# Fused two-stage attention and MLP on one core: a planner with other costs, joined filler matmuls, the last batch in token order, the last output tile in three pieces of columns

## The chip, the cores and the metric

The kernel runs on one core of one Trainium2 chip. The core has a matrix engine (TensorE, "PE" in the profile; its weight loads are "PEld"), a vector engine (DVE), an activation engine (ACT), GpSimd (POOL), SyncE (SP) and 16 DMA engines. The metric is device time in microseconds (us) of one execution, from one launch; lower is better. The time given for a kernel is the median of its runs.

## The reference

Eight batches, eight heads, 576 tokens of 64 numbers per head, and 32 "packed" queries `p` per head. The packed queries attend to the keys and values, then the queries attend to the packed result; the heads are put side by side to 512 columns, and an MLP with 2048 hidden columns (d_ff) follows:

```python
p_packed = sm_attn(p, k, v)            # softmax(p k^T / 8) v : 32 x 64 per head
out = sm_attn(q, p_packed, p_packed)   # softmax(q p_packed^T / 8) p_packed
x = out.transpose(0, 2, 1, 3).reshape(B * S, H * D)       # 4608 x 512
h = x @ w_in                                               # 4608 x 2048
g = where(h >= 1, h, where(h <= -1, 0, (h + 1)**2 / 4))
y = g @ w_out                                              # 4608 x 512, f32
```

## The kernel before

**Algebra.** The second attention and the first matmul of the MLP are merged: with A the normalised weights of the second softmax (transposed; 256 rows of head and packed query, in two groups g of 128) and M = p_packed w_in (256 x 2048), the hidden activations of a batch are M^T A. So per batch the kernel makes M and A, then 16 *hidden tiles* (`hidden_tile`, L541): tile `fi` is 128 columns of d_ff by the 576 tokens of the batch, four matmuls of 128x288 into PSUM (L548), `first` on ACT (L553, Prelu, PSUM to the f32 buffer `x`), `second` on DVE or ACT (L558 or L560), `third` on DVE (L563), which writes bf16 into `hT`. An *output tile* (`out_tile`, L584) is 128 tokens by 512 columns: 16 *steps*, one for each `fi`, each a 128x512 matmul that adds to one PSUM bank `o` (L598); then a copy to SBUF by ACT or DVE (`ob`, L319) and two DMAs on SP's queue (L604). Two batches share nine output tiles, so there are 36 of them and 576 steps.

**Attention of a batch** (`attention`, L357): `trans` (L376) turns k and q with matmuls on PE, twelve 96-wide ones for each half of the heads, for batches 0 to 2; from batch 3 on a transposing DMA on SP's queue does it (`turned`, L512). `scores` (L397, `sp`) and an exp on ACT (L400, `ex`); `packed` (L417 and L423, `pk`), a copy `p1`, an add and a copy that make `ppT` (L433, L435) and a reciprocal `rs` (L436); `weights` (L451, `s2`), exp on ACT (L456, `eT`), the sums (L461, `sm`), their reciprocal on ACT as ln and exp (L465, L469, `rc`) and `norm` on DVE (L472, `A`); `mk` (L493, `mp`) with a copy by ACT or DVE, which makes a quarter of M (M0 to M3, 512 columns of d_ff each). A hidden tile needs both groups of A and its quarter of M.

**Buffers.** `psW` has 3 PSUM buffers of two banks, which every product except `o` takes; `psO` has 2 banks for `o`. The `x` buffers are 5, the `ob` buffers 6. With two `o` banks, at most two output tiles are under way.

**Order.** All of the work is handed as tasks to a planner (`Plan`, L33), which is run when the program is built. It keeps a clock for each engine, takes the cost of each task and the delays between engines from the table `C` (L12), and picks the next task by start time and key; the order in which it picks is the order in which the instructions are emitted, and each engine works through its own in that order. So a change of a number in `C` can change the order of every engine's queue, but no instruction's duration on the chip. Loads go through POOL's queue in a fixed order: k, v and q of batch 0 in halves, w_in and w_out in quarters, k, v and q of batch 1, the last quarter of w_out, p, and then the later batches. While fewer than three `o` tiles have been begun and PE has nothing to do by the planner's clock, `run` (L131 to L139) emits *fillers*, 128x256 matmuls on zeros (L661), one for each 107 ns of planned idle time.

**Rows of the output.** A load puts six neighbouring tokens of a head into one partition, so the kernel's token order is not the output's: token 6t + 2e + x of a batch stands at x * 288 + e * 96 + t. `out_rows` (L573) cuts a tile into pieces in which t runs on, up to 96 rows, each of which is one DMA with every sixth row of the output as its target.

**The last output tile** (`end`, L588) has two accumulators of 256 columns, one in the bank of `o` and one in a `psW` buffer (`o2`), and each step is two 128x256 matmuls. `done_last` (L606) copies one half on ACT and one on DVE, and each of the two engines' queues (ACT's and SP's) sends two DMAs, of 96 and 32 rows.

## Time and profile before

| | |
|---|---|
| runs shown | 252.23 us median of three (251.41, 252.23, 252.58) |
| the profiled execution | 250.97 us, of which the span from the first to the last instruction is 249.2 us |
| PE, ACT, DVE busy | 94%, 73%, 73% of the span |
| granted clock of TensorE | 1.00 throughout |
| output DMAs | 72 issues on SP's queue and 2 on ACT's |

The profile is one execution. A row of a timeline or of the chain of waits gives the start in us from the span's start, the duration in us, the engine, the line of the kernel, the instruction and its tiles, and how many instructions are merged; in square brackets stands the engine's idle time before it and what ended it. A matmul's duration holds its way through the array, so the distance between two starts, and not the duration, is what a matmul costs in a stream of them.

### The profile page before, as it was taken

The numbers are of one execution on the slowest core, as the hardware profiler recorded it, in microseconds if no ns is written. First come the engines' busy times: TensorE is split into PE (matmuls) and PEld (weight loads), VectorE is DVE, ScalarE is ACT, GpSimd is POOL, SyncE is SP. The second block draws the span as 40 slices with busy tenths as digits, with TensorE's granted clock in tenths as the row PEclk, the third lists the DMA queues.
The fourth block names the chain that finished last, engine by engine and source line by source line (L and its number), as shares of the span: only waits on it lengthen the run. The fifth ranks groups of instructions, "written<-read, shape, count | busy, mean of one in ns | idle before, by whom it ended". The sixth has DMA issues, their size and how long they took to land.

```text
span 249.2 us, 5464 instructions
## 1 busy us (share of the span) xinstructions
PE 234.8 (94%) x2187; PEld 140.9 (57%) x2220; DVE 181.7 (73%) x308; ACT 182.5 (73%) x294; POOL 29.7 (12%) x44
## 2 busy tenths in 40 slices
PE   7887887999999999999999999999999999999993
PEld 5655465467546666556565656656556465544452
DVE  5456979788999899698979985998569878930000
ACT  3368888899888899798798984997859796841110
POOL 8632433012001301111101000000000000000000
PEclk9999999999999999999999999999999999999999
DMA  6999999999999999999999932312112112133223
GB/s 99 196 207 207 206 203 195 204 240 204 193 182 217 165 190 193 208 183 188 223 191 223 218 76 53 79 42 49 42 42 45 43 42 45 42 84 86 54 74 84
DMA packets 54825, 34.37 MB, mean 138 GB/s; under 512 B 27536, under 2 KB 50320, under 8 KB 54800
## 3 DMA queue, kind: packets, MB, share of 16 engines
q0 software_dynamic: 24672, 18.55, 49.9%
q1 hardware_dynamic: 29968, 15.34, 31.7%
q8 instruction: 17, 0.28, 0.4%
q10 hardware_dynamic: 160, 0.13, 0.2%
q14 instruction: 8, 0.07, 0.1%
HBM read 37.22 MB, written 9.44 MB: 187 GB/s over the span
## 4 chain that ended last, share of the span: by engine, by line
PE 76%; DMA 13%; ACT 3%; POOL 3%; issue 2%; DVE 2%; DVEq 0%; ACTq 0%; POOLq 0%
PE o L598 44%; PE h L548 22%; DMA w_in_sb<-in_moe_w_in_dram 7%; DMA q<-in_q_dram 6%; PE mp L493 3%; PE sp L397 2%; PE pk L417 1%; PE sm L461 1%; PE s L451 1%; PE tp L376 1%; DVE pT L319 1%; POOL w_in_sb L285 1%; ACT eT L456 1%; POOL k L259 1%; PE pk L423 1%
## 5 line engine op out<-in xcount | busy, mean ns | idle before, releaser
L598 PE MATMUL o<-w_out_sb,hT 128*128 128x512 bf16 (+1 forms) x559 | 135.6, 373 | 2.1 <-issue 1.1
L563 DVE SCALAR_TENSOR_TENSOR hT<-x 128x576 bf16<-128x576 f32 x128 | 93.2, 754 | 8.3 <-PE o L598 3.5
L598 PEld LDWEIGHTS <-hT 128*128 128x128 bf16 x592 | 56.1, 98 | 53.7 <-issue 4.8
L553 ACT ACTIVATE x<-h 128x576 f32<-128x576 f32 x128 | 77.2, 653 | 12.1 <-PE h L548 8.3
L548 PE MATMUL h<-A,M 128*128 128x288 bf16 x512 | 76.0, 286 | 1.4 <-ACT M L319 0.5
L548 PEld LDWEIGHTS <-M 128*128 128x128 bf16 x512 | 49.3, 98 | 24.1 <-ACT M L319 1.0
L558 DVE TENSOR_SCALAR x<-x 128x576 f32<-128x576 f32 x84 | 38.5, 459 | 11.8 <-ACT x L553 10.9
L319 ACT COPY ob<-o 128x512 f32<-128x512 f32 (+1 forms) x23 | 13.2, 576 | 32.1 <-PE o L598 32.1
L560 ACT ACTIVATE x<-x 128x576 f32<-128x576 f32 x44 | 29.4, 683 | 0.5
L319 DVE COPY ob<-o 128x512 f32<-128x512 f32 (+1 forms) x14 | 9.4, 669 | 25.8 <-PE o L598 25.7
L319 DVE CAST M<-mp 128x1024 bf16<-128x1024 f32 x16 | 19.4, 1218 | 2.8 <-PE mp L493 2.8
L319 ACT CAST M<-mp 128x1024 bf16<-128x1024 f32 x16 | 15.8, 1012 | 1.2 <-PE mp L493 1.2
L400 ACT ACTIVATE ex<-sp 96x768 bf16<-96x768 f32 x16 | 12.9, 806 | 3.2 <-PE sp L397 3.1
L472 DVE SCALAR_TENSOR_TENSOR A<-eT,rs,rc 128x576 bf16<-128x576 bf16 x16 | 13.0, 812 | 2.1 <-ACT rc L469 2.1
L259 POOL DMA_DIRECT2D k<-in_k_dram x10 | 7.5, 746 | 56.5 <-DMA kT<-k 40.0
L456 ACT ACTIVATE eT<-s,rs 128x576 bf16<-128x576 f32 x16 | 11.2, 736 | 2.8 <-PE s L451 2.6
L493 PE MATMUL mp<-w_in_sb,ppT 64*32 64x512 bf16 x256 | 10.7, 381 | 2.6 <-DMA w_in_sb<-in_moe_w_in_dram 2.2
L465 ACT ACTIVATE ln<-sm 128x576 f32<-128x576 f32 x16 | 10.4, 648 | 2.2 <-PE sm L461 2.1
L661 PE MATMUL o<-zeros 128*128 128x256 bf16 x68 | 10.6, 301 | 1.2 <-DVE zeros L247 1.2
L469 ACT ACTIVATE rc<-ln 128x576 f32<-128x576 f32 x16 | 10.9, 683 | 0.5
L259 POOL DMA_DIRECT2D q<-in_q_dram x10 | 7.6, 759 | 26.2 <-DMA qT<-q 12.7
L397 PEld LDWEIGHTS <-kT 128*128 128x128 bf16 x192 | 7.4, 98 | 2.6 <-DVE kT L319 0.6
(47 smaller groups left out, 114.4 us busy)
## 6 DMA issues: line engine op xcount, KB each, us to landing
out_dram<-ob SPq DMA_DIRECT2D x23, 192.0 KB, 2.5
v<-in_v_dram POOLq DMA_DIRECT2D x7, 576.0 KB, 18.4
k<-in_k_dram POOLq DMA_DIRECT2D x6, 576.0 KB, 12.4
q<-in_q_dram POOLq DMA_DIRECT2D x6, 576.0 KB, 14.0
out_dram<-ob SPq DMA_DIRECT2D x24, 128.0 KB, 2.8
w_in_sb<-in_moe_w_in_dram POOLq DMA_DIRECT2D x4, 512.0 KB, 14.7
w_out_sb<-in_moe_w_out_dram POOLq DMA_DIRECT2D x4, 512.0 KB, 16.8
out_dram<-ob SPq DMA_DIRECT2D x23, 64.0 KB, 2.0
```

Source lines behind the costliest of these rows:

```text
L259: nc.gpsimd.dma_start(tok[nm, b][:, hs].rearrange("p h c d -> p h (c d)"), SRC[nm][b, hs].rearrange("h (p c) d -> p h (c d)", c=NC))
L319: return lambda eng: nc.vector.tensor_copy(out_, in_) if eng == DVE else nc.scalar.copy(out_, in_)
L400: nc.scalar.activation(ex()[:, :, i].rearrange("p e x a n -> p e (x a n)"), box["sp"], AF.Exp, scale=scale)
L456: nc.scalar.activation(box["eT"], box["s2"][:, :, :HALF], AF.Exp, scale=rs()[:, g, 1:])
L472: nc.vector.scalar_tensor_tensor(A()[:, g], box["eT"], rs()[:, g, :1], box["rc"], ALU.mult, ALU.mult)
L493: nc.tensor.matmul(mp[a * NP:(a + 1) * NP, g], pp_of(y, h), w_in_sb[y * D:(y + 1) * D, h // 2, f * FW:(f + 1) * FW], start=True, stop=True)
L548: nc.tensor.matmul(h[:, hf, :HALF], T[b, "M"][:, g, fi * P:(fi + 1) * P], T[b, "A"][:, g, hf], start=(g == 0), stop=(g == G - 1))
L553: nc.scalar.activation(box["x"], box["h"][:, :, :HALF], AF.Prelu, bias=-1.0, alpha=0.5)
L558: nc.vector.tensor_scalar(x, x, 1.0, 0.0, ALU.add, ALU.max)
L560: nc.scalar.activation(x, x, AF.Relu, bias=1.0)
L563: nc.vector.scalar_tensor_tensor(hT[:, fi, col:col + S].rearrange("p (a t) -> p a t", a=2), box["x"], 1.0, box["x"], ALU.min, ALU.mult)
L598: nc.tensor.matmul(o, hT[:, fi, i * P:(i + 1) * P], w_out_sb[:, fi, cs], start=(fi == 0), stop=(fi == KF - 1))
```

## The change

1. **The planner's table.** `C` gets other numbers. Among them: `load` 2.95 to 3.5666, `land` 1.75 to 2.0125, `xt` 5 to 6.5, `M` 0.345 to 0.2415, `s2` 0.25 to 0.2862, `pk` 1.05 to 0.9765, `td` 0.457 to 0.489, `obd` 0.69 to 0.6276, `slack` 0.6 to 0.51, `margin` 0.15 to 0.1717, `feed` 0.1 to 0.085, `join` 0.15 to 0.1604. All of the other entries but `tell` (0.04 to 0.034) stay.
2. **Fillers.** Planned idle time is counted up and emitted ahead of PE's next task as matmuls of up to 512 columns.
3. **Last batch.** `norm` of batch 7 is two DVE instructions (one for each x) that write A in the order t, e, so that its columns are in the order of the tokens; `out_rows` then cuts at 288 rather than 96, and a DMA writes every second row of the output.
4. **Last tile.** The left 256 columns are summed first, in 16 steps, copied and sent; then the right 256 in 16 steps of two 128-column matmuls each, into two banks of one `psW` buffer, and two copies of 128 columns with one DMA each.
5. A list `cuts` is made for the first four output tiles. No other line reads it.

```diff
-C = dict(load=2.95, half=1.46, w_in=2.57, w_out=2.57, rest=1.25, out=9.0, p=4.05, land=1.75, xt=5.0, xland=11.0,
...
+C = dict(load=3.5666, half=1.46, w_in=2.57, w_out=2.57, rest=1.25, out=9, p=4.05, land=2.0125, xt=6.5, xland=11, tpp=0.06, tp=0.042, sc=0.034, pk=0.9765, s2=0.2862, sm=0.245, M=0.2415, h=0.49, o=0.217, switch=0.05, join=0.1604, pTc=0.1, Tca=1.12, Tcd=0.76, ex=0.82, ppT=0.42, ppo=0.41, ppa=0.4, ppd=0.2, rs=0.18, eT=0.74, ln=0.65, rc=0.68, A=0.82, Mca=1, Mcd=1.22, x=0.65, ta=0.683, td=0.489, hT=0.758, oba=0.585, obd=0.6276, array=0.2, wake=1.2, warm=4.2, early=0.3, tell=0.034, feed=0.085, slack=0.51, margin=0.1717, wait=0.5)
-DW = 256
+DW, FILL = 256, 512
...
-                    idle()
+                    fill += DW
                     self.now["PE"] += step
                     continue
...
+            while e == "PE" and fill:
+                w = min(fill, FILL)
+                idle(w)
+                fill -= w
...
             def norm(eng):
+                if b == B - 1:
+
+                    for x in range(X):
+                        o, e, r_ = [v.rearrange(w, e=E) for v, w in ((A()[:, g, x], "p (t e) -> p t e"),
+                                    (box["eT"][:, x], "p (e t) -> p t e"), (box["rc"][:, x], "p (e t) -> p t e"))]
+                        nc.vector.scalar_tensor_tensor(o, e, rs()[:, g, :1], r_, ALU.mult, ALU.mult)
+                    return
                 nc.vector.scalar_tensor_tensor(A()[:, g], box["eT"], rs()[:, g, :1], box["rc"], ALU.mult, ALU.mult)
...
+            if b == B - 1:
+                r = t % HALF
+                n = min(HALF - r, (i + 1) * P - t)
+                res.append((t - i * P, n, out[b * S:(b + 1) * S].rearrange("(r x) d -> x r d", x=X)[x, r:r + n]))
+                t += n
+                continue
...
-        w = d_model // 2
+
+        cuts = [12, KF] if pr == 0 and i < 4 else [KF]
+
+        w, sub = (d_model // 2, d_model // 4) if end else (d_model, d_model)
...
-            box["o2"] = wide([P, w], f32, "o2")
+            box["o2"] = wide([P, 2, FW], f32, "o2")
...
+            pieces = [(box["o2"][:, y, :sub], slice(w + y * sub, w + (y + 1) * sub)) for y in range(2)] if j else [(box["o"][:, :w], slice(w))]
+            for o, cs in pieces:
                 nc.tensor.matmul(o, hT[:, fi, i * P:(i + 1) * P], w_out_sb[:, fi, cs], start=(fi == 0), stop=(fi == KF - 1))
...
+            for y, (eng, queue) in enumerate(((ACT, nc.scalar), (DVE, nc.sync))):
+                ob = ops.tile([P, sub], f32, tag="ob" + str(y), name="ob" + str(y), bufs=1)
+                copy(ob, box["o2"][:, y, :sub])(eng)
+                for a, n, dst in out_rows(pr, i):
+                    queue.dma_start(dst[:, w + y * sub:w + (y + 1) * sub], ob[a:a + n])
+        for j in range(2 if end else 1):
+            if j:
+                prev = prev + [add(PE, 0.0, 100 + pr * NT + i, prev, spare, takes="W", readers=1)]
+            for fi in range(KF):
+                t = add(PE, C["o"] * (0.5 if end else 1.0), 100 + pr * NT + i, [wrote[b, fi] for b in bs] + prev + [L["out", fi // 4]],
+                        lambda fi=fi, j=j: step(fi, j), mode=0, takes="O" if fi == 0 and j == 0 else None, readers=1, slack=C["slack"])
...
+            if j:
+                add((DVE, ACT), {ACT: C["oba"], DVE: C["obd"]}, b_key(pr, i), prev, done_last)
+            else:
+                both(done, C["oba"], C["obd"], b_key(pr, i), prev, frees=owner, takes="ob", holds=C["out"])
```

The order that the planner makes of it, as far as the prediction speaks of it (instructions of PE in the order of its queue; "steps" are those of output tiles):

| stretch | before | after |
|---|---|---|
| fillers | 68 of 256 columns | 33 of 512 and 6 of 256 |
| ahead of the first turn of k of batch 1 | 12 hidden tiles, 18 steps | 15 hidden tiles, 17 steps |
| then, up to `pk` of batch 1 | turn, 2 tiles, turn, `sp`, step, tile, `sp`, tile, 5 steps | turn, tile, 3 steps, turn, step, `sp`, 3 steps, `sp` |
| after `pk` of batch 1 | turn q, turn q, M0, s2, s2, sm, M1, sm, step, M2, 2 steps, M3 | turn q, M0, turn q, s2, M1, M2, s2, sm, M3, step, sm |
| ACT after the exps of `sp` of batch 1 | p1, q copy, eT, eT, ln, rc, ln, rc | p1, ppT copy, M0 copy, eT, M1 copy, eT, ln, rc, ln, rc |
| steps ahead of the first hidden tile of batch 1 | 40 | 36 |
| steps between the first `s2` and the first hidden tile, batches 2 to 7 | 24, 23 and 6 tiles, 25 and 7 tiles, 21 and 6 tiles, 17, 20 | 24, 22, 22, 22, 24, 23 |

More of the change, by code (lines that the diff above doesn't have):

```diff
@@ L123, in run @@
                     given[e].append(t)
-        n = len(self.tasks)
+        n, fill = len(self.tasks), 0
         while n:
@@ L478, in weights @@
             i_ = add(ACT, C["rc"], km, [l_] + p_, inv)
-            a_ = add(DVE, C["A"], km, [i_] + K.get((b - 2, "h"), []), norm)
+            a_ = add(DVE, C["A"] + (0.1 if b == B - 1 else 0.0), km, [i_] + K.get((b - 2, "h"), []), norm)
             last["ln"] = [i_]
@@ L601, in done @@
             box["ob"] = ops.tile([P, d_model], f32, tag="ob", name="ob")
-            copy(box["ob"], box["o"])(eng)
+            copy(box["ob"][:, :w], box["o"][:, :w])(eng)
             for a, n, dst in out_rows(pr, i):
-                nc.sync.dma_start(dst, box["ob"][a:a + n])
+                nc.sync.dma_start(dst[:, :w], box["ob"][a:a + n, :w])
         def done_last(eng):
-            for j, (eng, queue, o) in enumerate(((ACT, nc.scalar, box["o"][:, :w]), (DVE, nc.sync, box["o2"]))):
-                ob = ops.tile([P, w], f32, tag="ob" + str(j), name="ob" + str(j), bufs=1)
-                copy(ob, o)(eng)
-                for a, n, dst in sorted(out_rows(pr, i), key=lambda x: -x[1]):
-                    queue.dma_start(dst[:, j * w:(j + 1) * w], ob[a:a + n])
@@ L613, in out_tile @@
-        if end:
-            prev = [add(PE, 0.0, 100 + pr * NT + i, [K[B - 1, "h"][-1]], spare, takes="W", readers=1)]
-        for fi in range(KF):
-            t = add(PE, C["o"], 100 + pr * NT + i, [wrote[b, fi] for b in bs] + prev + [L["out", fi // 4]],
-                    lambda fi=fi: step(fi), mode=0, takes="O" if fi == 0 else None, readers=1, slack=C["slack"])
-            step_of[pr, i, fi] = t
-            prev = [t]
-            if fi == 0:
-                owner = t
-        both(done_last if end else done, C["oba"], C["obd"], b_key(pr, i), prev, frees=owner, takes="ob", holds=C["out"])
+            for y, (eng, queue) in enumerate(((ACT, nc.scalar), (DVE, nc.sync))):
[3 more added lines that the diff above has]
+                    queue.dma_start(dst[:, w + y * sub:w + (y + 1) * sub], ob[a:a + n])
@@ L660 @@
     plan.count["O"] = 1
-    plan.run(lambda: nc.tensor.matmul(o[:, :DW], zeros[:, :P], zeros[:, :DW], start=True, stop=True))
+    plan.run(lambda w: nc.tensor.matmul(o[:, :w], zeros[:, :P], zeros[:, :w], start=True, stop=True))
 _INS = ['q', 'k', 'v', 'p', 'moe_w_in', 'moe_w_out']
```

13 lines of the change are left out of this document (6 added, 7 removed).

## The prediction

> **What bounds the kernel now.** I read the sums and groups of the page, then busy time in stretches of 10 us, then the chain of waits.
>
> ```profile
> span 249.2 us, 5464 instructions
> PE 234.8 (94%) x2187; PEld 140.9 (57%) x2220; DVE 181.7 (73%) x308; ACT 182.5 (73%) x294; POOL 29.7 (12%) x44
> ...
> 20.00:30.00 10.00, 8.38 (x65) 5.30 (x63) 8.03 (x15) 8.66 (x15) 2.56 (x5) 1.00 1.24 207
> 30.00:40.00 10.00, 9.32 (x137) 6.42 (x137) 8.39 (x14) 8.43 (x14) 4.07 (x5) 1.00 1.31 204
> 40.00:50.00 10.00, 8.30 (x107) 4.50 (x106) 8.36 (x13) 8.12 (x12) 1.53 (x2) 1.00 1.44 197
> 60.00:70.00 10.00, 9.79 (x82) 5.84 (x82) 9.27 (x18) 8.76 (x15) 0.45 (x1) 1.00 1.27 206
> 200.00:210.00 10.00, 9.95 (x76) 5.92 (x62) 7.57 (x13) 7.66 (x13) 0.00 (x0) 1.00 0.22 54
> ...
> 179.22 1.96 PE h L548 x16
> 192.00 3.45 PE o L598 x16
> 219.22 10.74 PE o L598 x49
> 240.80 4.53 PE o L598 x36
> ```
>
> The columns of the stretches are length, then busy time of PE, PEld, DVE, ACT and POOL, clock, DMA share and GB/s. From about 53 us on PE is 98 to 99% busy and the chain's rows follow one another on it; the last 26 us hold only steps. There the time is the count of matmuls by their spacing: a step 3.45 / 16 = 0.216 us, a hidden tile 1.96 / 4 = 0.49 us. The kernel computes as much as before, so these 190 us can't shrink by a new order; they can only get gaps. What can be won or lost lies in the first 53 us, where PE is idle (1.6, 0.7 and 1.7 us in three of the stretches), and behind the last matmul.
>
> **The first 53 us.** Loads set this part, and POOL's queue has the same order in both kernels, so I keep their landings. The rows of before:
>
> ```profile
> 25.07 0.41 PE L493 MATMUL mp<-w_in_sb,ppT 64*32 64x512 bf16 x8 [0.98 <-DMA w_in_sb<-in_moe_w_in_dram]
> 28.51 1.64 PE L548 MATMUL h<-A,M 128*128 128x288 bf16 x12 [0.49 <-ACT M L319]
> 33.59 0.68 PE L376 MATMUL tp<-ident,k 96*128 96x96 bf16 x12 [0.51 <-DMA k<-in_k_dram]
> 38.61 0.86 PE L417 MATMUL pk<-ex,v 96*128 96x64 bf16 x24
> 40.86 0.68 PE L376 MATMUL tp<-ident,q 96*128 96x96 bf16 x12 [0.58 <-DMA q<-in_q_dram]
> 49.05 0.65 PE L548 MATMUL h<-A,M 128*128 128x288 bf16 x4
> ...
> 51.38 0.51 PE tp L376 x12
> 55.52 0.35 PE sp L397 x12
> ...
> L560 ACT ACTIVATE x<-x 128x576 f32<-128x576 f32 x44 | 29.4, 683 | 0.5
> 37.44 0.80 ACT L400 ACTIVATE ex<-sp 96x768 bf16<-96x768 f32 x1
> 39.79 0.37 ACT L319 COPY p<-pk 64x256 f32<-64x256 f32 x1 [0.30 <-PE pk L423]
> 42.08 1.49 ACT L456 ACTIVATE eT<-s,rs 128x576 bf16<-128x576 f32 x2 [0.64 <-PE s L451]
> 48.00 1.02 ACT L319 CAST M<-mp 128x1024 bf16<-128x1024 f32 x1
> ...
> 46.25 0.82 DVE L472 SCALAR_TENSOR_TENSOR A<-eT,rs,rc 128x576 bf16<-128x576 bf16 x1 [0.25 <-ACT rc L469]
> ```
>
> *Up to 33.6 us.* In the new order the copy of M2 comes earlier in ACT's queue, the wait of 0.49 us at 28.51 goes, and 15 tiles and 17 steps instead of 12 and 18 stand ahead of the first turn of k. That turn waits for its load in both. So PE is ahead by 3 x 0.49 - 0.216 = 1.25 us of work.
>
> *Up to pk.* Before: 38.61 - 33.59 = 5.0 us of queue without a gap. After: two turns (0.51), one tile, seven steps and two `sp` (0.35) make 3.7 us, so PE stands at `pk` at about 37.3. But ACT's exps are no earlier: the first `sp` ends at about 36.5, then ACT does exp (0.80), a relu of a hidden tile (0.68) and exp, 36.5 + 2.3 less 0.1, by which a next one starts before an end, = 38.7. Half of `pk` needs the second exp. Nearly all of the 1.25 us is idle time here; `pk` ends at 39.4.
>
> *The second half of q.* It lands at about 40.8 (row 40.86). Before, its turn follows the first one. Now M0 stands ahead of it, and M0 waits for `ppT`: p1 (0.37), an add on DVE and a copy on ACT of about the same size, one behind the other from 39.5 on, with 0.1 between them 40.9. M0 takes 0.3 to the next start; the turn begins at 41.2, 0.3 later, and behind it in PE's queue everything else.
>
> *ACT's queue.* Now the copies of M0 and M1 (0.9 each to the next start, row 48.00) lie ahead of the first and the second `eT`. First `eT` 41.35 + 0.9 = 42.3 (42.08 before), second 43.9 (42.08 + 1.49 / 2 = 42.8 before), and from there ln, rc, ln, rc as before: A is complete at about 48.5 instead of 47.07. PE fills this with the 12 steps that are left, but with one gap, where the third output tile waits for an `ob` copy that stands behind two M copies on DVE. The first hidden tile of batch 1 then starts at about 48.7 with 36 steps done; before, at 49.05 with 40. Behind by 4 x 0.216 - 0.35 = 0.5 us.
>
> I take **+0.5 us**. Ends: -1.5, if the 1.25 us and one switch of tiling (about 0.28) are kept because ACT's exps do come earlier; +1.5, if A's delay of 1.4 us shows in full.
>
> **From 53 us to 219 us.** From batch 3 on each attention moves some 5 to 9 us of PE's work later, and no hidden tiles are left between `s2` and the first tile that needs A. By counts and spacings the distance is 22 steps, 4.75 us, and 1.1 us of other matmuls, 5.85 us for batches 3 to 5 (before 9 to 10). Is the chain shorter? Batch 6 of before had 17 steps and four M products:
>
> ```profile
> 167.64 0.37 PE s L451 x16
> 173.49 0.98 PE h L548 x8
> qT<-q SPq DMA_TRANSPOSE x10, 8.1
> ...
> 169.69 0.65 ACT L465 ACTIVATE ln<-sm 128x576 f32<-128x576 f32 x1 [0.36 <-PE sm L461]
> 172.49 0.82 DVE L472 SCALAR_TENSOR_TENSOR A<-eT,rs,rc 128x576 bf16<-128x576 bf16 x1 [0.58 <-ACT rc L469]
> ```
>
> From `s2` to the end of A it took 173.31 - 167.64 = 5.67 us, to the tile 5.85, without a wait of PE. The new batches have the same distance, so 0.2 us to spare: I take **+0.1** for all, 0 to +2 as ends (0.4 for each of five batches). The turning DMAs go out later on SP's queue, the second q of batch 4 behind output tile 9; that is still 20 us of PE's queue ahead of its `s2`, and a landing takes 8.
>
> **Fillers.** 72 x 256 columns instead of 68. Ahead of loads they end where the load lands; one unit more delays batch 0's A by 0.1 us, which the wait of 0.98 us at 25.07 takes up: 0. Without that wait 0.1.
>
> The rows for the two edits at the end:
>
> ```profile
> 245.25 0.37 ACT L319 COPY ob<-o 128x256 f32<-128x256 f32 x1 [2.75 <-PE o L598]
> 245.36 0.42 DVE L319 COPY ob<-o 128x256 f32<-128x256 f32 x1 [24.50 <-PE o L598]
> 245.65 0.86 ACTq L612 DMA_DIRECT2D out_dram<-ob  x2
> 245.81 0.79 SPq L612 DMA_DIRECT2D out_dram<-ob  x2
> L319 DVE COPY ob<-o 128x512 f32<-128x512 f32 (+1 forms) x14 | 9.4, 669 | 25.8 <-PE o L598 25.7
> ...
> out_dram<-ob SPq DMA_DIRECT2D x1, 96.0 KB, 2.1
> ...
> 45.89 0.51 PE L331 MATMUL tpp<-ident,p_nat 128*128 128x128 bf16 x6
> 46.24 2.97 PE L598 MATMUL o<-w_out_sb,hT 128*128 128x512 bf16 x13
> 5.07 0.28 DVE L319 COPY pT<-tpp 64x256 bf16<-64x256 bf16 x1 [0.79 <-ACT pT L319]
> ...
> L598 PEld LDWEIGHTS <-hT 128*128 128x128 bf16 x592 | 56.1, 98 | 53.7 <-issue 4.8
> ```
>
> **Last batch.** `norm` takes 0.82 us for 576 columns. Two halves pay the fixed part twice; by DVE's copies of 512 and 256 columns (0.67 and 0.42 us) that part is 0.17 us. Reading with a stride has no row: 0 to 0.8 us for each group. Batch 7 has 23 steps between `s2` and its tiles, so a part is covered: **+0.1**, ends 0 and +1.
>
> **The tail.** The 32 matmuls of 256 columns become 16 of 256 and 32 of 128. Six of 128 columns, each with its weight load, took 46.24 - 45.89 = 0.35 us, 0.058 each; 256 columns take half a step, 0.108. 32 x 0.058 - 16 x 0.108 = +0.1. The copies shrink to 128 columns (0.12 us less than 256 by DVE's copies: 0.25 us on ACT, 0.30 on DVE), but both read one `psW` buffer, and the row at 5.07 shows DVE beginning a copy of such a buffer only where ACT's ends. So the DVE copy ends at 245.25 + 0.25 + 0.04 + 0.30 = 245.84 instead of 245.78. One DMA of 128 rows instead of two, whose second went out 0.4 us behind the first: -0.4. Sum -0.4 + 0.06 + 0.1 = **-0.25 us**; ends -0.5 (copies side by side) and +1.
>
> The Trainium skill ("TensorE: Matmul & The Clock Gate", Back-to-back issue gap) says that in a stream of weight load and matmul pairs a 128-column matmul is spaced by some 81 ns; by that the tail would be +0.5. The row at 45.89, such a stream, has 58 ns and decides.
>
> **Splitting d_ff.** `cuts` is read nowhere: 0.
>
> Sum: 0.5 + 0.1 + 0.1 - 0.25 = +0.45, so 251.4 us against the profiled execution's own 250.97 (span 249.2 and 1.8 around it). That execution lies 1.26 below the median of the runs, which a single run may; to the median the sum gives 252.23 + 0.4 = 252.6 us.
>
> **The rivals.**
> - *The work done early is kept.* ACT's exps come sooner, or PE finds steps at `pk`, and the order after `pk` costs nothing: -1.25 - 0.28 - 0.25 = -1.8, 250.5 us. For it: 1.25 us of idle time goes by 33.6 us. Against: in both orders the 24 steps that two `o` banks and three quarters of w_out allow are done by `pk`, so no step is left to fill with. 0.17.
> - *Late attention stalls PE* (slower): in batches 3 to 7 A comes after the steps are used up, because an `ob` copy (0.67 us) stands ahead of A on DVE. It decides from a chain of 5.85 us on; at 6.25, 5 x 0.4 = 2.0 on top: 254.6 us. For it: 0.2 us to spare. Against: batch 6 of before. 0.25.
> - *128-column matmuls bound by their weight load*: the load's own row is 98 ns, so 32 x 0.04 = 1.3 us more, 253.9 us. 0.05.
>
> **How the numbers follow.** The forecast has 0.53, its own range 251.5 to 253.6. Half a percent is 1.26 us, about what a measurement here can tell from no change: below 250.97 is faster, above 253.49 slower. The forecast gives 0.46 within and 0.07 slower, the first rival 0.14 faster and 0.03 within, the second 0.22 slower and 0.03 within, the third 0.03 slower and 0.02 within. Faster 0.14, same 0.54, slower 0.32. The range takes in the first rival's lower half and the second's price: 250.6 to 254.6.
>
> **What would show it.** `pk` of batch 1 with a gap of about 1 us that ACT's exp ends; the second turn of q at 41.2; A of batch 1 complete at 48.5; the first hidden tile at 48.7. PE without gaps over 0.2 us ahead of the hidden tiles of batches 3 to 7. The last DMA landing 2.6 us behind the last matmul, DVE's copy behind ACT's. The forecast is wrong if PE's idle time between 34 and 53 us doesn't grow, or if any wait of PE for A beyond 60 us exceeds 0.4 us.

## The result and the profile after

| | before | after |
|---|---|---|
| runs, median (lowest to highest) | 251.82 us (251.10 to 252.84, 6 runs) | 254.23 us (253.37 to 256.83, 6 runs) |
| after to before | | 1.0102, 95% interval 1.0066 to 1.0137 |
| profiled execution, span | 250.97 us, 249.2 us | 253.37 us, 251.6 us |
| first `s2` of batch 2 | 67.89 us | 69.40 us |
| end of the last matmul | 245.32 us | 248.12 us |
| end of the last DMA | 248.21 us | 250.43 us |

The kernel became slower by 1.0%, and the whole interval lies beyond the half percent that counts as a change. The forecast was 252.6 us with no change as the likeliest outcome (slower had 0.32). The time is inside the range of 250.6 to 254.6 us, near its upper end; the sum behind the forecast was too small. A ratio here and below compares executions made side by side and leaves out those more than 1.5% above a kernel's fastest, so it is not the quotient of two medians.

The last three rows of the table split the 2.4 us between the two profiled executions (up to the first `s2` of batch 2 both orders hold the same work, 71 steps and 32 hidden tiles): 69.40 - 67.89 = +1.51 us up to the first `s2` of batch 2 (the head), 178.72 - 177.43 = +1.29 us from there to the last matmul (the middle), and 2.31 - 2.89 = -0.58 us from there to the last landing, of which 0.17 comes back after the landing (the span ends 1.17 us behind it, 1.00 before): -0.41 us (the tail).

The first part of the page of after:

```profile
span 251.6 us, 5460 instructions
...
PE 239.4 (95%) x2207; PEld 139.0 (55%) x2207; DVE 178.8 (71%) x310; ACT 185.4 (74%) x295; POOL 29.4 (12%) x44
...
L556 PE MATMUL h<-A,M 128*128 128x288 bf16 x512 | 76.3, 286 | 1.7 <-ACT x L561 1.7
```

PE still sets the end. What is new is in the last row: 1.7 us in which a hidden tile waits for ACT. Busy time by stretches (columns as in the prediction), after:

```profile
30.00:40.00 10.00, 9.27 (x137) 6.66 (x130) 9.18 (x16) 7.83 (x12) 4.15 (x5) 1.00 1.31 203
40.00:50.00 10.00, 8.15 (x105) 4.39 (x103) 7.13 (x11) 7.95 (x13) 1.53 (x2) 1.00 1.44 198
50.00:60.00 10.00, 8.84 (x127) 6.69 (x127) 8.13 (x14) 9.68 (x15) 1.51 (x2) 1.00 1.28 226
60.00:70.00 10.00, 10.00 (x96) 6.00 (x92) 9.07 (x18) 7.97 (x15) 0.81 (x2) 1.00 1.27 208
```

and the one stretch of before that the prediction did not show:

```profile
50.00:60.00 10.00, 9.60 (x140) 7.26 (x141) 8.80 (x15) 9.83 (x15) 1.87 (x3) 1.00 1.29 227
```

Between 50 and 60 us PE lost 0.76 us, outside the stretch that the prediction walked through. The timeline of PE, ACT and DVE, ahead of that and in it, after:

```profile
29.87 0.41 PE L501 MATMUL mp<-w_in_sb,ppT 64*32 64x512 bf16 x8 [1.01 <-DMA w_in_sb<-in_moe_w_in_dram]
...
33.91 0.68 PE L377 MATMUL tp<-ident,k 96*128 96x96 bf16 x12
...
38.97 0.51 PE L418 MATMUL pk<-ex,v 96*128 96x64 bf16 x12 [0.73 <-ACT ex L401]
...
40.73 0.84 PE L501 MATMUL mp<-w_in_sb,ppT 64*32 64x512 bf16 x8 [0.45 <-DVE ppT L434]
41.50 0.68 PE L377 MATMUL tp<-ident,q 96*128 96x96 bf16 x12
...
48.23 0.79 ACT L320 COPY pT<-tpp 64x768 bf16<-64x768 bf16 x1
48.83 0.65 PE L556 MATMUL h<-A,M 128*128 128x288 bf16 x4
49.06 0.55 DVE L320 COPY pT<-tpp 64x768 bf16<-64x768 bf16 x1 [0.41 <-ACT pT L320]
49.64 0.80 ACT L320 COPY pT<-tpp 64x768 bf16<-64x768 bf16 x1 [0.62 <-DVE pT L320]
50.46 0.65 ACT L561 ACTIVATE x<-h 128x576 f32<-128x576 f32 x1
50.47 0.56 DVE L320 COPY pT<-tpp 64x768 bf16<-64x768 bf16 x1 [0.86 <-ACT pT L320]
51.16 0.65 PE L556 MATMUL h<-A,M 128*128 128x288 bf16 x4 [1.17 <-ACT x L561]
```

The rows at 38.97 and 40.73 are gaps that were foreseen; the first two and the lower ones were not. The packed queries of the later batches are turned into one buffer `tpp`, and four copies empty it into `pT`. In the new order two of them are on ACT and two on DVE, by turns, and each starts within 0.04 us of the end of the one on the other engine: the four follow one another from 48.23 to 51.03 us. The `first` of hidden tile 1 (the ACTIVATE at 50.46) stands behind ACT's second copy. PE has no free `psW` buffer until it is done, and the second hidden tile waits 1.17 us.

In the middle no wait of PE for A appears. The waits of ACT between 60 and 219 us, in us in total, how often, and the longest, after:

```profile
ACT x L561 <- DVE hT L571: 4.9, 11, 0.6
```

Before, this row was 2.4 us in 3 waits. One such place in the timeline of after:

```profile
134.64 0.76 DVE L571 SCALAR_TENSOR_TENSOR hT<-x 128x576 bf16<-128x576 f32 x1
...
135.49 0.65 ACT L561 ACTIVATE x<-h 128x576 f32<-128x576 f32 x1 [0.58 <-DVE hT L571]
...
136.20 0.65 PE L556 MATMUL h<-A,M 128*128 128x288 bf16 x4 [0.51 <-ACT x L561]
```

The five `x` buffers are all taken: `first` on ACT waits until `third` on DVE has emptied one (134.64 + 0.76 = 135.40), and PE waits for the PSUM buffer that `first` empties. Most of these waits are too short to show as a gap of PE; they show in the distance from one matmul's start to the next, which in the middle is longer than the usual one by 1.5 us in sum ahead of hidden tiles (0.4 us in `e2_rest_alone`, 0.7 us in `e5_x_buffers`, both below).

The end, after:

```profile
246.42 0.37 ACT L320 COPY ob<-o 128x256 f32<-128x256 f32 x1 [1.16 <-PE o L616]
248.16 0.27 ACT L320 COPY ob<-o 128x128 f32<-128x128 f32 x1 [1.37 <-PE o L616]
248.46 0.37 ACTq L629 DMA_DIRECT2D out_dram<-ob  x1
248.46 0.29 DVE L320 COPY ob<-o 128x128 f32<-128x128 f32 x1 [21.92 <-ACT ob L320]
248.78 0.33 SPq L629 DMA_DIRECT2D out_dram<-ob  x1
```

The first copy starts when 16 matmuls of 256 columns are done, the second when 32 of 128 columns are: 248.16 - 246.42 = 1.74 us, 0.054 us for each. DVE's copy begins where ACT's ends, and the last DMA lands at 250.43 us, 1.65 us after its issue.

### The profile page after: what moved, and what is told of

Read it like the earlier page. It is cut to its first block, busy times and chain, and to the rows that moved or that the text cites. A ratio compares the mean times of both kernels' runs of the same rounds, so it can differ in the third digit from the quotient of the medians.

```text
span 251.6 us, 5460 instructions
## 1 busy us (share of the span) xinstructions
PE 239.4 (95%) x2207; PEld 139.0 (55%) x2207; DVE 178.8 (71%) x310; ACT 185.4 (74%) x295; POOL 29.4 (12%) x44
## 4 chain that ended last, share of the span: by engine, by line
PE 77%; DMA 10%; ACT 5%; DVE 4%; issue 1%; POOL 1%; DVEq 0%; ACTq 0%; POOLq 0%
PE o L616 47%; PE h L556 20%; DMA w_in_sb<-in_moe_w_in_dram 8%; PE mp L501 3%; DMA k<-in_k_dram 3%; DVE hT L571 2%; PE sp L398 1%; PE pk L418 1%; ACT x L561 1%; PE sm L462 1%; DVE x L566 1%; PE tp L377 1%; PE s L452 1%; ACT M L320 1%; ACT pT L320 1%
## 5 line engine op out<-in xcount | busy, mean ns | idle before, releaser
L616 PE MATMUL o<-w_out_sb,hT 128*128 128x512 bf16 (+2 forms) x608 | 143.8, 368 | 0.5 <-DVE ob L320 0.3
L571 DVE SCALAR_TENSOR_TENSOR hT<-x 128x576 bf16<-128x576 f32 x128 | 94.9, 756 | 6.3 <-ACT x L568 1.1
L561 ACT ACTIVATE x<-h 128x576 f32<-128x576 f32 x128 | 78.3, 654 | 13.9 <-PE h L556 7.4
L566 DVE TENSOR_SCALAR x<-x 128x576 f32<-128x576 f32 x90 | 40.9, 455 | 10.1 <-ACT x L561 10.0
L320 ACT COPY ob<-o 128x512 f32<-128x512 f32 (+2 forms) x24 | 13.5, 564 | 25.7 <-PE o L616 25.5
L568 ACT ACTIVATE x<-x 128x576 f32<-128x576 f32 x38 | 25.7, 682 | 0.1
L320 ACT CAST M<-mp 128x1024 bf16<-128x1024 f32 x22 | 21.5, 1019 | 3.1 <-PE mp L501 3.1
L320 DVE CAST M<-mp 128x1024 bf16<-128x1024 f32 x10 | 12.2, 1222 | 6.2 <-PE mp L501 6.2
L480 DVE SCALAR_TENSOR_TENSOR A<-eT,rs,rc 128x576 bf16<-128x576 bf16 x14 | 11.3, 814 | 7.3 <-ACT rc L470 7.3
L682 PE MATMUL o<-zeros 128*128 128x512 bf16 (+1 forms) x39 | 11.3, 419 | 1.2 <-DVE zeros L248 1.2
```

What stands on the lines that cost most here:

```text
L320: return lambda eng: nc.vector.tensor_copy(out_, in_) if eng == DVE else nc.scalar.copy(out_, in_)
L480: nc.vector.scalar_tensor_tensor(A()[:, g], box["eT"], rs()[:, g, :1], box["rc"], ALU.mult, ALU.mult)
L561: nc.scalar.activation(box["x"], box["h"][:, :, :HALF], AF.Prelu, bias=-1.0, alpha=0.5)
L566: nc.vector.tensor_scalar(x, x, 1.0, 0.0, ALU.add, ALU.max)
L568: nc.scalar.activation(x, x, AF.Relu, bias=1.0)
L571: nc.vector.scalar_tensor_tensor(hT[:, fi, col:col + S].rearrange("p (a t) -> p a t", a=2), box["x"], 1.0, box["x"], ALU.min, ALU.mult)
```

## The experiments

Where a run's "stretch" is spoken of, it is the middle: from the first `s2` of batch 2 to the end of the last matmul (177.43 us before, 178.72 us after).

### Which edit: the table, or all the rest

`e1_table_alone` is the kernel before with the new numbers of `C` and nothing else; `e2_rest_alone` is the kernel after with the old numbers, the other half of the same cut. The first of them:

```diff
-C = dict(load=2.95, half=1.46, w_in=2.57, w_out=2.57, rest=1.25, out=9.0, p=4.05, land=1.75, xt=5.0, xland=11.0,
-         tpp=0.06, tp=0.042, sc=0.034, pk=1.05, s2=0.25, sm=0.245, M=0.345, h=0.49, o=0.217, switch=0.05, join=0.15,
+C = dict(load=3.5666, half=1.46, w_in=2.57, w_out=2.57, rest=1.25, out=9.0, p=4.05, land=2.0125, xt=6.5, xland=11.0,
+         tpp=0.06, tp=0.042, sc=0.034, pk=0.9765, s2=0.2862, sm=0.245, M=0.2415, h=0.49, o=0.217, switch=0.05, join=0.1604,
...
```

> The kernel before with the new table C alone: old fillers, old norm, old last tile. Theory 'order': the order that the table makes costs all of the loss and more. Up to the first s2 of batch 2 (69.40 us after, 67.89 before) 1.5 us, from there to the last matmul another 1.3, and the tail isn't shortened, so +2.8 us against before, last matmul at about 248.1, last matmul to end 3.9 us. Rival 'other edits': fillers, norm or last tile cost the time, and the table alone is within 0.5 us of before.

> The changed kernel with the old table: joined fillers, last batch in token order, last tile in three pieces, in the order of before. Theory 'order': -0.4 us against before, all of it behind the last matmul (3.47 us instead of 3.88), last matmul at 245.3. Rival 'other edits': +2 us or more, with a wait of PE ahead of batch 7's hidden tiles or around the fillers.

The table alone: 255.23 us, ratio 1.0145 (1.0109 to 1.0182), first `s2` of batch 2 at 69.96 us and a stretch of 179.11 us. The rest alone: 252.39 us, ratio 1.0020 (0.9985 to 1.0055), 68.37 us and 177.47 us. So both losses come with the order that the table makes, and in the profiled execution fillers, last norm and last tile add nothing in the middle (177.47 against 177.43 us). The 0.48 us by which `e2_rest_alone` is late at the first `s2` of batch 2 is as much as its second half of q landed later (41.29 against 40.81 us). Six of the twelve executions of `e2_rest_alone` took 250.9 to 251.6 us, the profiled one among them, the other six 253.2 to 255.2; what these share was not found, it is why the interval is wide, and it leaves open whether the rest costs something in half of the executions.

### Which part of the order: the late attentions, the `x` buffers, the copies of `pT`

`xt` is the planner's cost of a turning DMA, and the one number that alone moves the attentions of batches 3 to 7 later. `e3_after_xt5` sets it back in the kernel after (6.5 to 5), `e4_before_xt65` brings it into the kernel before:

```diff
-C = dict(load=2.95, half=1.46, w_in=2.57, w_out=2.57, rest=1.25, out=9.0, p=4.05, land=1.75, xt=5.0, xland=11.0,
+C = dict(load=2.95, half=1.46, w_in=2.57, w_out=2.57, rest=1.25, out=9.0, p=4.05, land=1.75, xt=6.5, xland=11.0,
```

> The changed kernel with xt back at 5: the queues up to the first hidden tile of batch 1 are those of the changed kernel (M0 ahead of the second turn of q, 36 steps), but from batch 3 on the attentions stand 4 to 7 us earlier in PE's queue, as in the kernel before or nearly. Theory 'two places': the first part keeps its +1.5 us, the 1.3 us of the middle go, the tail gives -0.4: +1.1 us against before. Rival 'one place' (the late start of batch 1 alone makes the middle late too): +2.4, as the changed kernel. Rival 'middle alone': -0.4.

> The kernel before with xt 6.5 alone: the queues up to the first hidden tile of batch 1 are those of before (40 steps), but from batch 3 on each attention stands 4 to 10 us later, as in the changed kernel. Theory 'two places': first s2 of batch 2 at 67.9 as before, then 1.3 us of waits of PE for psW buffers in bursts of hidden tiles: +1.3 us. Rival: the late place costs nothing, 0.

`e4_before_xt65`: 251.92 us, ratio 1.0021 (0.9996 to 1.0046), stretch 177.63 us. Late attentions alone cost 0.2 us of the 1.29, and not the 1.3 expected. (Its first `s2` of batch 2 stands at 69.01 us instead of 67.9; PE was at half clock for 3.4 us ahead of it, see below.) `e3_after_xt5`: 253.33 us, ratio 1.0087 (1.0053 to 1.0122), so setting it back takes back little, if anything; +1.1 us was expected. (Its profiled execution had a wait of 4.0 us for a load of k that no other has, so its stretch is not compared.)

`e5_x_buffers` takes the kernel after in the same order, with four more `x` buffers that the planner does not know of; `e6_pT_on_DVE` puts the four `pT` copies of the later batches on DVE:

```diff
-    el = ctx.enter_context(tc.tile_pool(name="el", bufs=NX))
+    el = ctx.enter_context(tc.tile_pool(name="el", bufs=NX + 4))
```

```diff
-                                                            box["tp"][c * D:(c + 1) * D, :n])(eng),
+                                                            box["tp"][c * D:(c + 1) * D, :n])(eng if cast else DVE),
```

> The changed kernel with nine x buffers in SBUF instead of five; the planner still counts five, and the queues of all engines are the same. Theory 'bursts': from the first s2 of batch 2 to the last matmul the changed kernel is 1.3 us longer than before (178.7 us against 177.4) because in bursts of hidden tiles ACT waits for an x buffer and PE for a psW buffer behind it; with nine buffers ACT doesn't wait, so about -1 us against the changed kernel, +1.5 us against before, and this stretch 177.7 us. Rival 'psW': the three psW buffers or ACT's own work set it, and nothing changes: +2.5 us.

> The changed kernel with all four copies of the second pT on DVE instead of two on ACT and two on DVE in turn; the other instructions keep their order. Theory 'copies in turn': ACT's second copy waits for DVE's, the relu of batch 1's first tile stands behind it in ACT's queue, and PE waits 1.17 us for that tile's psW buffer (51.16 us). Without it PE waits at most 0.3 us there, so -0.8 us against the changed kernel, +1.7 us against before. Rival: DVE, with two more copies of 0.55 us, is late for batch 1's hidden tiles, and the time stays (+2.5 us).

`e5_x_buffers`: 253.42 us, ratio 1.0063 (1.0031 to 1.0095), stretch 177.73 us: 0.99 us of the 1.29 are gone, and with them all of ACT's waits for `hT` between 60 and 219 us. (By the times alone the gain is not clear of the noise: the intervals of this ratio, of the next one and of after overlap.) The tile that waited at 136.20 us, in the timeline of `e5_x_buffers`:

```profile
135.60 0.51 PE L398 MATMUL sp<-pT,kT 128*128 128x64 bf16 x12
...
135.95 0.65 PE L556 MATMUL h<-A,M 128*128 128x288 bf16 x4
```

`e6_pT_on_DVE`: 253.27 us, ratio 1.0061 (1.0030 to 1.0093), first `s2` of batch 2 at 68.41 us, 0.99 us earlier, stretch 179.13 us, 0.41 longer. (One of its twelve executions took 493.95 us at full clock; it is not in the ratio, and why is not known.) Its timeline:

```profile
48.28 2.25 DVE L320 COPY pT<-tpp 64x768 bf16<-64x768 bf16 x4
48.55 0.65 PE L556 MATMUL h<-A,M 128*128 128x288 bf16 x4
...
49.24 0.65 ACT L561 ACTIVATE x<-h 128x576 f32<-128x576 f32 x1 [1.19 <-PE h L556]
...
49.94 0.65 PE L556 MATMUL h<-A,M 128*128 128x288 bf16 x4 [0.23 <-ACT x L561]
```

On one engine the four copies are over in 2.25 us instead of 2.80, and ACT's `first` follows its hidden tile at once: the wait of 1.17 us is 0.23. Not all of the 0.99 us is due to this: the hidden tile ahead of the wait starts 0.28 us earlier too (48.55 against 48.83), in an execution whose last quarter of w_in landed 0.32 us earlier (29.51 against 29.83). About 0.7 us is left for the copies, and 0.4 is lost again in the middle, where no trace shows why.

`e12_both` has both mends.

> The changed kernel with both mends at once: nine instead of five x buffers, and the pT copies of one tpp buffer all on DVE. Theory (the two losses are separate: 1 us of the head by the copies in turn, 1 us of the middle by x buffers that come free late): both are won, first s2 of batch 2 at 68.4 us, from there to the last matmul 177.7 us, time 1.001 to 1.004 of the kernel before, that is level with it. Rival (one loss, seen at two places: ACT and DVE have too little time left in all, and what is won at one place is lost at the other): no better than each mend alone, 1.006.

252.98 us, ratio 1.0036 (1.0011 to 1.0062): better than each alone, short of the sum. Ten of its twelve executions had a lower mean granted clock than 0.995; the other two took 251.61 and 252.26 us, 1.000 and 1.003 of the median of the kernel before beside it, where the theory had put it. The stretch of its profiled execution is 177.34 us. The next experiment is about the ten.

### The granted clock in the head

The profiled execution of `e12_both` in short stretches (the seventh number, behind the five engines, is the granted clock):

```profile
40.50:41.00 0.50, 0.27 (x1) 0.09 (x1) 0.50 (x2) 0.29 (x1) 0.00 (x0) 1.00 1.28 213
41.00:41.50 0.50, 0.45 (x8) 0.11 (x7) 0.34 (x1) 0.12 (x1) 0.00 (x0) 0.99 1.23 197
41.50:42.00 0.50, 0.50 (x14) 0.49 (x8) 0.00 (x0) 0.36 (x1) 0.00 (x0) 0.50 1.69 205
...
47.50:48.00 0.50, 0.50 (x7) 0.50 (x6) 0.50 (x1) 0.47 (x2) 0.00 (x0) 0.50 1.32 206
48.00:48.50 0.50, 0.50 (x4) 0.19 (x2) 0.08 (x1) 0.50 (x1) 0.00 (x0) 0.68 1.31 203
48.50:49.00 0.50, 0.50 (x5) 0.20 (x3) 0.23 (x1) 0.04 (x1) 0.00 (x0) 1.00 1.30 200
```

PE ran at half clock from 41.5 to 48.3 us, right behind two gaps, in its timeline:

```profile
38.97 0.51 PE L418 MATMUL pk<-ex,v 96*128 96x64 bf16 x12 [0.52 <-ACT ex L401]
...
40.73 0.84 PE L501 MATMUL mp<-w_in_sb,ppT 64*32 64x512 bf16 x8 [0.44 <-DVE ppT L434]
```

In the profiled execution of `e4_before_xt65` PE was at half clock from 43.6 to 47.0 us. Over all executions the mean clock lies mostly near 1.000, 0.993 or 0.986; a step of 0.007 is 0.007 x 250 / 0.5 = 3.5 us at half clock. (Up to 0.003 more is lost where the clock falls behind the last matmul, in `e12_both` at 249.7 us, so 0.995 parts the executions with a step from those without.) The kernel before has it too: of the 88 executions that ran beside the experiments 48 lie at 0.995 and over (median 251.2 us), 31 between 0.988 and 0.995 (252.2) and 9 below (253.1). So a step costs 1.0 us.

`e13_filled` is `e12_both` with 16 matmuls on zeros, four of 256 columns ahead of each half of `pk`, of M0 and of the first `sm` of batch 1. They are no part of the computation:

```diff
+        def fill(o):
+            for _ in range(4 if b == 1 else 0):
+                nc.tensor.matmul(o, zeros[:, :P], zeros[:, :256], start=True, stop=True)
...
                 mp = box["mp"] = wide([P, G, FW], f32, "mp")
+                if f == 0:
+                    fill(mp[:, 0, :256])
```

> e12_both with 16 matmuls on zeros in batch 1's attention, four of 256 columns (0.44 us at full clock) ahead of each half of pk, of M0 and of the first sm, into PSUM that the real matmuls overwrite or nobody reads: PE's idle time between 38 and 45 us is filled, nothing else is changed. In e12_both 11 of 12 executions had a mean granted clock below 0.999, in steps of about 0.007, which is 3.4 us at half clock each; the profiled one had half clock from 41.4 to 48.3 us. Theory (the half clock comes from PE's idle time in this stretch): at most 3 of the executions below 0.995, median 251.3 to 252.2 us, ratio 0.999 to 1.003 although the fillers themselves may cost some tenths. Rival (the half clock has another cause, or the fillers cost as much as they bring): more than half of the executions below 0.995, 252.5 to 253.5 us.

251.88 us, ratio 1.0011 (0.9990 to 1.0031). None of its twelve executions is below a clock of 0.999 (`e12_both`: 10 of 12 below 0.995); the kernel before had 7 of 17 below 0.995 beside it. PE's busy time (the second number) from 38 to 45 us, in `e12_both`:

```profile
38.00:45.00 7.00, 5.52 (x102) 3.47 (x102) 4.81 (x9) 4.60 (x8) 2.30 (x3) 0.75 1.49 196
```

and in `e13_filled`:

```profile
38.00:45.00 7.00, 6.09 (x117) 4.04 (x114) 5.23 (x9) 4.91 (x8) 2.31 (x3) 1.00 1.49 196
```

So it is work that PE lacks in this stretch, the lack brings the half clock, and work of no use saves 1.1 us of the median. Level with before is not the same as nothing lost: the ten executions of the kernel before that ran beside it at full clock have a median of 251.24 us, 0.6 less. In the trace of `e13_filled` the head is still 0.96 us longer than before (68.85 against 67.89), the middle 0.1 shorter (177.34) and the tail 0.41 shorter. The busy time of `e12_both` is even flattered, since half of it was spent at half clock.

### The last tile: two buffers, and the sum in two parts of d_ff

The changed kernel makes a list `cuts` and does not use it. `e9_after_cuts` puts it to use: the first four output tiles are summed over 12 of the 16 parts of d_ff, copied to SBUF, and the rest is added by DVE; so a bank of `o` comes free before the last quarter of w_out has landed. The table is the new one. `e8_cuts` has the same with the old table, and gives each of the last two pieces of columns a `psW` buffer of its own.

```diff
+            def keep(eng):
+                box["half"] = const.tile([P, d_model], f32, name="half" + str(i))
+                copy(box["half"], box["o"])(eng)
+
+            def join(eng):
+                box["ob"] = ops.tile([P, d_model], f32, tag="ob", name="ob")
+                nc.vector.tensor_tensor(box["ob"], box["o"], box["half"], ALU.add)
...
-            box["o2"] = wide([P, 2, FW], f32, "o2")
+            box["o2"] = [wide([P, FW], f32, "o2" + str(y)) for y in range(2)]
```

(The last two lines are in `e8_cuts` alone.)

> The old table, joined fillers, last batch in token order, last tile in three pieces in two psW buffers, and the first four output tiles summed in two parts, d_ff tiles 0 to 11 and 12 to 15, with a copy to SBUF between them and an add on DVE behind. 52 steps instead of 40 stand ahead of batch 1's first hidden tile. Theory 'no steps to fill with': between 34 and 49 us PE is idle for 3 us because 24 steps are all that two o banks allow; here 12 more fill it: -2 us against before. Rival 'engines full': the four more copies and slower adds on ACT and DVE delay A of batch 1 by as much, 0 or slower.

> The changed kernel with the list cuts put to use (first four output tiles in two parts, as in the run with the old table), new table, last tile as in the change. 52 steps instead of 36 stand ahead of batch 1's first hidden tile. Theory 'missing part': the new table's loss in the first 70 us (1.1 to 1.5 us) goes, because what it lacks are steps for PE's queue; the middle keeps its 1.3 us: about +0.5 us against before. Rival 'order': +2.5 us as the changed kernel.

`e8_cuts`: 254.54 us, ratio 1.0104 (1.0073 to 1.0135). `e9_after_cuts`: 249.54 us, ratio 0.9898 (0.9859 to 0.9937), faster than both kernels. PE in the timeline of `e9_after_cuts`:

```profile
36.87 1.46 PE L634 MATMUL o<-w_out_sb,hT 128*128 128x512 bf16 x6
...
38.52 1.46 PE L634 MATMUL o<-w_out_sb,hT 128*128 128x512 bf16 x6
39.81 0.86 PE L418 MATMUL pk<-ex,v 96*128 96x64 bf16 x24
...
41.33 1.46 PE L634 MATMUL o<-w_out_sb,hT 128*128 128x512 bf16 x6
...
49.44 0.65 PE L556 MATMUL h<-A,M 128*128 128x288 bf16 x4 [0.47 <-ACT M L320]
```

Where after waits for the exp, for `ppT` and for ACT's copies, there are now steps: PE is busy for all of the 7 us from 38 to 45 (4.68 after), 52 steps instead of 36 are done ahead of the first hidden tile of batch 1, and none of six executions has a clock below 0.997. All of the gain is in the head: at the first `s2` of batch 2 (68.45 us, 0.95 earlier) 85 steps are done instead of 71, which is 14 x 0.216 = 3.0 us of work. The stretch from there (175.82 us) is 2.9 us shorter than after because it holds these 14 steps less, so the loss of the middle is still in it. The old table does not use the room (2 us less than before were expected): in `e8_cuts` DVE empties two `kT` buffers ahead of the first hidden tile, which starts 2.9 us later than in `e9_after_cuts`:

```profile
51.52 1.42 DVE L320 COPY kT<-tp 128x1152 bf16<-128x1152 bf16 x2
52.33 0.65 PE L556 MATMUL h<-A,M 128*128 128x288 bf16 x4 [1.66 <-DVE kT L320]
...
248.27 0.27 ACT L320 COPY ob<-o 128x128 f32<-128x128 f32 x1 [1.31 <-PE o L616]
248.32 0.29 DVE L320 COPY ob<-o 128x128 f32<-128x128 f32 x1 [24.54 <-PE o L616]
```

That is about half of what parts the two. From the first `s2` of batch 2 on, `e8_cuts` takes 177.95 us against 175.82, with 476 steps against 475; PE waits there 1.0 us for an exp, 0.9 for a turned k and 0.5 for M.

The last two rows answer for the two buffers: the copies now run side by side, and DVE's ends 0.34 us after the start of ACT's instead of 0.59. But the last landing came 2.04 us after its issue instead of 1.65, and the tail was no shorter (3.57 us from the last matmul to the end of the span, 3.47 in after). This is one profile, but no scatter: in all ten traces in which DVE's copy of the new last tile stands behind ACT's, the last landing takes 1.64 to 1.66 us. In `e8_cuts` the two DMAs go out 0.08 us apart instead of 0.32; that this makes the last one slower is likely, but was not tested.

### The best version

`e10_cuts_x` is `e9_after_cuts` with seven `x` buffers, for which the halves are kept as bf16 (two more would not fit otherwise); `e11_cuts_x_pT` also has the `pT` copies on DVE.

```diff
-    el = ctx.enter_context(tc.tile_pool(name="el", bufs=NX))
+    el = ctx.enter_context(tc.tile_pool(name="el", bufs=NX + 2))
...
-                box["half"] = const.tile([P, d_model], f32, name="half" + str(i))
+                box["half"] = const.tile([P, d_model], bf16, name="half" + str(i))
```

> The changed kernel with the first four output tiles really summed in two parts of d_ff (e9_after_cuts), two more x buffers (seven) to which the halves kept as bf16 give the room. Theory (the middle's bursts of hidden tiles are limited by x buffers there too): stretch from the first s2 of batch 2 to the last matmul shorter than the 175.8 us of e9_after_cuts by 0.3 to 0.6 us, time 0.986 to 0.988 of the kernel before. Rival (with the sums split DVE and ACT have less slack in the middle than buffers can mend): no change, 0.990.

> As e10_cuts_x, and the pT copies of one tpp buffer all on DVE. Theory (copies of one PSUM buffer on two engines go in turn, and a relu on ACT waits behind them): the wait of PE for ACT at about 51 us goes, first s2 of batch 2 earlier by up to 0.9 us, time 0.982 to 0.987. Rival (that time is covered by the steps that this kernel has there): as e10_cuts_x.

`e10_cuts_x`: 249.03 us, ratio 0.9885 (0.9857 to 0.9913), stretch 175.54 us against 175.82. `e11_cuts_x_pT`: 249.10 us, ratio 0.9884 (0.9855 to 0.9913), stretch 175.55 us. Both are level with `e9_after_cuts` within the intervals. The `pT` copies on DVE bring nothing here: first `s2` of batch 2 at 68.54 against 68.27 us, since steps stand where PE would wait. In 18 executions of these three kernels the clock is never below 0.997, and each kernel's times lie within 0.65 us; those of after lie within 3.5.

## Why the prediction was right, and where its sum failed

The time is in the range, and that is in part luck: the upper end was the price of PE waiting for A in the middle, which did not happen, and the sum itself gave +0.45 us where the profiled executions are 2.4 apart. Of the signs, PE's idle time between 34 and 53 us did grow (19 us with 16.89 busy before, 15.26 after), and no wait for A beyond 60 us exceeded 0.4 us, since there was none.

- *Up to 33.6 us: work done early, and the turn of k waits for its load in both.* The second half failed. The turn starts at 33.91 us without a gap, 0.56 us behind the landing of its load (33.35 us) and 0.32 later than before: PE had waited 1.01 us for the last quarter of w_in (row 29.87), a wait that the walk did not have.
- *Work done early is lost at `pk`, the walk from 33.6 to 48.7 us.* Right in its places, though A at 48.5 does not follow from the terms given (the second `eT` 1.1 us later makes 47.07 + 1.1 = 48.2): `pk` waits 0.73 us for the second exp, M0 for `ppT`, the second turn of q starts at 41.50 (forecast 41.2), A is complete at 47.84 + 0.81 = 48.65 (48.5), the first hidden tile starts at 48.83 (48.7). Behind by 4 steps less 0.22 us, 0.64 against the forecast 0.5.
- *Head +0.5.* The mechanism held, the term was too small: +1.51. The walk ended at the first hidden tile, and the next wait stood one tile further on: 1.17 us at 51.16, because the four `pT` copies go by turns on ACT and DVE. The order showed these copies; the prediction had even read from the row at 5.07 that DVE begins such a copy where ACT's ends, and used it for the tail alone. With the copies on one engine the head is +0.52, or about +0.8 if the landings were those of after. The step that failed is the size of this term: the walk ended one tile too early and left this wait at nothing without a reason.
- *Middle +0.1, by the chain from `s2` to A.* That chain costs nothing, as forecast: no wait of PE for A beyond 60 us. But it was the wrong thing to look at. The term is +1.29 us, and 0.99 of it comes from `x` buffers that come free late in runs of hidden tiles, a wait that the prediction has at nothing; the late attentions alone cost 0.2. Which numbers of the table bring these runs was not tested. The second rival (254.6 us) had the size and not the mechanism.
- *Fillers 0, `cuts` 0.* The joined fillers are not free at their place: in after the first turn of k starts at 6.81 us without a gap, 0.72 behind its landing. A later wait for a load covers it (1.24 us for w_in at 17.08). Both held as far as the profiled execution of the rest alone shows, which loses nothing in the head but what q landed later.
- *Last batch +0.1.* Covered. The term of one group is larger than the 0.17 us that was taken:

```profile
L480 DVE SCALAR_TENSOR_TENSOR A<-eT,rs,rc x14: 798/817/820, 15.6 to 180.3; 128x576 bf16<-128x576 bf16 x14
L478 DVE SCALAR_TENSOR_TENSOR A<-eT,rs,rc x4: 539/548/554, 206.2 to 208.1; 128x288 bf16<-128x288 bf16 x4
```

  The columns in the middle are the shortest, the median and the longest in ns. Two halves take 2 x 548 = 1096 ns, 0.28 us more than 817; by the fixed part alone it would be 0.17, so the strided reading and the other order of writing cost about 0.1 together. No instruction of PE waited for it.
- *Tail -0.25.* It was -0.41. DVE's copy stands behind ACT's as forecast. One DMA instead of two saves 0.21 us of the 0.34 taken (-0.4 + 0.06) up to its issue: the last one goes out 0.66 us behind the last matmul instead of 0.87. That it then lands after 1.65 us instead of 2.02 was not in the sum. The 128-column matmuls are spaced by 0.054 us, so 32 of them cost no more than 16 of 256 columns: 1.74 against 16 x 0.108 = 1.73 us, where +0.1 was taken. The Trainium skill's 81 ns ("TensorE: Matmul & The Clock Gate", Back-to-back issue gap) is not what this stream shows, nor is a bound by the weight load, the third rival.
- *The rivals.* The first (work kept, 250.5 us) is what happens once PE has steps at `pk`: `e9_after_cuts`. In the changed kernel there are none, as the argument against it said. No row shows the 0.28 us that this rival and the lower end of the head take for a switch of tiling: in the trace of before the distance from a step to a matmul of 64 rows behind it is 0.309 us instead of 0.216, so 0.09 for the switch.

## What to carry to other kernels

When an order moves, follow the walk until the queues of all engines are level again, not until the first instruction that the change was about: here the largest wait behind the loads stood one tile behind the point where the sum stopped. Look also at copies that empty one PSUM buffer on two engines: here they went by turns, 2.80 us for four against 2.25 on one, and a hidden tile's `first` stood behind them. And if the times of one kernel scatter in steps, look at the granted clock by execution and at the stretch where PE idles in small pieces: filling these, with work moved there or even with matmuls on zeros, took the scatter away here.

## What the runs showed of the hardware

The half clock needs no long pause of PE: the longest gap in the 3.4 us ahead of it in `e12_both` is 0.52 us. How much of 38 to 45 us PE was busy does not decide it alone either. With 5.5 us of 7 in `e12_both` 10 of 12 executions had it, with 4.9 in `e5_x_buffers` 6 of 12, with 4.7 in after 1 of 6; with 6.1 in `e13_filled` and 7.0 in `e9_after_cuts` none of 12 and none of 6. An idle stretch does it as well: in `e3_after_xt5` PE waited 3.99 us for a load, up to 144.25 us, and had half clock from 144.3 to 147.7.

What does part the stretches is how much of the array the matmuls use. In all fourteen traces the changes of the clock stand on a grid of 3.41 us. For each window of the grid, add up rows x columns x moving columns of the matmuls that start in it, as a share of what steps in a row (128*128, 512 columns each 0.216 us) would make. The 17 windows with half clock behind them, most of them after the last matmul, have a share of 0.34 or less (0.29 in `e12_both` from 38.1 us, 0.34 in `e4_before_xt65` from 40.2 us); the 985 other windows at full clock have 0.37 or more (0.37 in `e13_filled` from 40.7 us, one of the lowest). PE was busy for 70% and 64% of the first two windows, and for 63 to 66% of several that kept the clock: matmuls of 64 rows and 32 columns, or of 64 moving columns, keep PE busy and count for little here.

The 3.41 us agree with the window of some 3.4 us, running free of the kernel's start, that the Trainium skill gives ("TensorE: Matmul & The Clock Gate", Part 1: The HAM clock gate); in the fourteen traces the first window at full clock begins 3.95 to 7.23 us after the start. Its table asks for an idle window, as in `e3_after_xt5`; the drops in `e12_both` and `e4_before_xt65` came without one, and its section on a second failure mode of the gate, many small pauses (A second HAM failure mode: psum-queue depth-cycling), fits them better. Where the grid falls would then decide which executions are hit. Laid over the matmuls of `e12_both` as they ran, every place of the grid has a window of 0.34 or less, and 10 of 12 executions were hit; over those of `e9_after_cuts` no place has less than 0.43, and none was. For the kernel before the same working gives a tenth of the places, where 40 of 88 executions were hit, so something is still missing from it.

The head moves with the landings of the loads too: after and `e5_x_buffers`, with one order and full clock, had their first `s2` of batch 2 at 69.40 and 69.94 us, 0.54 apart, and the last quarter of w_in landed at 29.83 and 30.36 us, 0.53 apart. And three of the six executions of after took 254.2 to 254.4 us at full clock, some 0.9 above the profiled one; where these spend it, no trace shows.
